# Attention units of 64 tokens of two batches, in array quarters, in place of 128 tokens of one

## The chip, the cores and the metric

The kernel runs on one core of a Trainium2 chip, as one program. The metric is the device time of a run in microseconds. All times below are of that one core.

## The reference

A linear attention with a decaying state, then two feed-forward layers. The first layer is a leaky rectifier with a slope per feature, the second the mish function.

```python
for t in range(S):                      # B, H, S, D = 4, 8, 768, 48
    cur = np.einsum('bhd,bhe->bhde', u[None] * kt, vt)
    y[:, :, t] = np.einsum('bhd,bhde->bhe', rt, state + cur)
    state = w[None, :, :, None] * state + np.einsum('bhd,bhe->bhde', kt, vt)
x = y as (3072, 384)
x = (relu(x @ w_in) + alpha * min(x @ w_in, 0)) @ w_out      # 384 -> 2048 -> 384
x = mish(x @ w2_in) @ w2_out                                 # 384 -> 2048 -> 384
```

## The kernel before

The sequence is cut into six chunks of 128 tokens. A unit of attention is one chunk of one batch, with all eight heads: 24 units, four to a block, blocks zero to five. Unit u is batch u % 4 of chunk u // 4. A block of four units gives 512 tokens of x, and the first layer works on 512 tokens at a time.

Inside a unit the decay is put into r and k beforehand (prep_rk multiplies both with the table RK). Then the unit is: the carried state T times r (first loop of batch, L324), scores k times r (L296, written for the unit after), which a masked copy on VectorE (L300) puts into A above a diagonal that ScalarE presets (L284), the unit's contribution to the state (L334; the keys for it are scaled with the table Kn on GpSimd, L276), and v times A (L339), which adds onto the carried part in the same PSUM banks. The two heads of a pair lie at partitions 0 to 47 and 64 to 111, so that carried state and scores run in quarters of the TensorE array (64 rows by 64 columns), four at a time; the state and v times A contract over 128 tokens and run in two halves. All these matmuls are in fp32, and each is shown by the trace as two records.

Afterwards t_decay (L345) and t_update (L352) bring T up to date on VectorE, x_parts splits y into a high and a low part (ScalarE L70, VectorE L73), and six small DMAs move the heads of the last pair into place in x. Block zero has functions of its own (c_first, attend0, x_first, states_first).

The first layer has 96 slots, six blocks times 16 weight blocks. A slot is nine matmuls into h (L144), the activation (L426, L428), its split (L70, L73) and nine matmuls into acc (L458) for the slot two before. In the first 16 slots each slot also prepares its weights: ScalarE scales (L96, L97), VectorE joins (L102) and takes the low part (L73), and the high part is a cast on ScalarE or GpSimd (L113).

The order of all this is written out by hand: `at(place, work, ...)` puts a step at a place counted in slots, and the steps run in the order of their places. Block zero's places are the table E, those of every later unit come from the offsets K in plan_unit, and AT gives each unit's slot: 2 for unit four, 5 for unit five, then one every four slots. The engines work through their instructions in that order. Loads stand on SyncE's queue (SP) in the same order. nat holds r, k and v of a unit by token; its three buffers set when the next load can start, and on GpSimd prep_c multiplies r, u and k (L267, L268).

```python
at(s + 0.60, batch, u)
at(s + 0.61, t_decay, u)
at(s + K["t"], t_update, u)
at(s + K["x"], x_parts, u)
```

Of the kernel before, what the change touches and what calls it, by code (L numbers as in the profile page):

```python
# [30 lines left out]
C = 128  # L31
# [12 lines left out]
UNITS = [(b, j) for j in range(NCH) for b in range(B)]  # L44
BLOCKS = [UNITS[4 * j:4 * j + 4] for j in range(NCH)]

# [5 lines left out]
def attention_and_two_ff(ctx: ExitStack, tc, rkT, nat, wT, ub, consts, w1, w2, alphaT, out):  # L52
# [99 lines left out]
    cst = att.tile([128, (1 + NPR) * C], F32, name="cst")  # L152
# [5 lines left out]
    inp = {}  # L158
    vz_t = {}

# [7 lines left out]
    def load_unit(u):  # L168
        if u < B:
            f = NF - 2 * B + 2 * u  # L170
            rk = per.tile([PR, 2, NPR, C], F32, tag=f"w{f}", name=f"w{f}u")
            n = per.tile([128, 4, DM], F32, tag=f"w{f + 1}", name=f"w{f + 1}u")
            by_seat(rk, rkT[u], slice(None))
            dma.dma_start(out=n[:, 1:3], in_=nat[u, :, 1:3])
            inp[u] = (rk, n, n[:, 2])
            vz_t[u] = n[:, 3].rearrange("s (q c e) -> s q c e", q=2, c=KC)
            return
        a = att.tile([PR, 2, NPR, C], F32, tag="rk", name="rk", bufs=3)
        by_seat(a, rkT[u], slice(None))
        n = att.tile([128, 3, DM], F32, tag="nat", name="nat", bufs=3)  # L180
        dma.dma_start(out=n, in_=nat[u])
        inp[u] = (a, n, n[:, 2])
# [3 lines left out]
    w128 = att.tile([PR, NPR], F32, name="w128")  # L186
    Kn = att.tile([128, NPR, 2, D], F32, name="Kn")
    T = att.tile([PR, B, NPR, 64], F32, name="T")
    def tables():
# [27 lines left out]
        mul(w128, iG[:, :, 0], G[:, :, 8])  # L217
        mul(uw, uw, wide(wt, 2))

    def table_Kn():  # L220
        kw = new("m")[0:PR].rearrange("d (p s) -> d p s", p=NPR)
        t = bank("acc2")
        for p in range(NPR):
            act.activation(out=kw[:, p, :], in_=RK[:, 1, p, :], func=AF.Copy, scale=w128[:, p:p + 1])
            pe.transpose(t[:, p * C:p * C + PR], kw[:, p, :], ident[:PR, :PR])
# [3 lines left out]


# [4 lines left out]
    LAST = (1, 2)  # L235
# [42 lines left out]
    def preset(u, h):  # L278

        if h == 0:  # L280
            A_t[u] = att.tile([128, 2, NPR, C], F32, tag="A", name="A", bufs=2)
        for j in range(NPR):
            p, q = HEAD[h, j]
            act.activation(out=A_t[u][:, h, j, :], in_=ident, func=AF.Copy, scale=c_t[u][1][:, 2 * p + q, :])  # L284

    def scores(u):

        rk = inp[u][0]
        if u == 0:
            sc_t["banks"] = [bank("sc", 2) for h in range(2)]  # L290
        sc_t[u] = sc_t["banks"]
        for j in range(NPR):
            for half in (1, 0):
                t0 = 64 * half if u else 0
                for h in range(2):
                    pe.matmul(sc_t[u][h][HALF[half], j * C + t0:(j + 1) * C], rk[ROWS[h], 1, j, HALF[half]],  # L296
                              rk[ROWS[h], 0, j, t0:], start=True, stop=True)

    def masked(u, q):
        dve.copy_predicated(A_t[u][:, q].rearrange("s p t -> s (p t)"), mask, sc_t[u][q])  # L300
# [13 lines left out]
    def batch(u):  # L314


        b, j = UNITS[u]
        rk, n, v = inp[u]
        A = A_t.pop(u)
        y = yt_t[u] = [bank("yt"), bank("h", 2)]  # L320
        for r in range(2):
            for h, q in ((0, 0), (1, 1), (0, 1), (1, 0)):
                i = 2 * q + r
                pe.matmul(y[h][64 * q:64 * q + 64, r * C:(r + 1) * C], T[ROWS[h], b, i, :], rk[ROWS[h], 0, i, :],  # L324
                          start=(r == 0), stop=False)
        if u + 1 < NU:
            scores(u + 1)
        if j < NCH - 1:
            st_t[u] = y[0][:, 2 * C:2 * C + NPR * D]
            for i in range(NPR):  # L330
                for h in range(2):
                    p, q = HEAD[h, i]
                    o = (2 * p + q) * D
                    pe.matmul(st_t[u][ROWS[h], i * D:(i + 1) * D], n[:, 1, o:o + D], v[:, o:o + D], start=False, stop=False)  # L334
        for p in PAIR:
            for q in range(2):
                o = (2 * p + q) * D
                h, i = SEAT[p, q]
                pe.matmul(y[h][ROWS[q], p % 2 * C:(p % 2 + 1) * C], v[:, o:o + D], A[:, h, i, :],  # L339
                          start=False, stop=(p in LAST))  # L340

    def t_decay(u):
        b, j = UNITS[u]
        if j < NCH - 1:
            dve.tensor_tensor(out=T[:, b, :, 0:D], in0=T[:, b, :, 0:D], in1=w128.unsqueeze(2).to_broadcast([PR, NPR, D]), op=ALU.mult)  # L345

    def t_update(u):
        b, j = UNITS[u]
        if j < NCH - 1:
# [35 lines left out]
    def x_parts(u):  # L385

        y = yt_t.pop(u)
        hi, lo = x_of(u)
        y3 = att.tile([128, 2, C], F32R, tag="y3", name="y3", bufs=1)
        parts = [(y3[0:PR, 0], y3[0:PR, 1], y[1][0:PR, C:2 * C]), (hi[0:PR, 2], lo[0:PR, 2], y[1][0:PR, 0:C]),  # L390
                 (hi[0:PR, 0:2], lo[0:PR, 0:2], y[0][0:PR, 0:2 * C].rearrange("d (c t) -> d c t", c=2))]
# [4 lines left out]
        x = x_t[u // 4][:, :, :, u % 4 * C:(u % 4 + 1) * C].bitcast(F32)  # L396
        for q in range(2):
            for c in range(KC):
                dma.dma_start(out=x[48 + 64 * q:64 + 64 * q, :, c, :],
                              in_=y3[64 * q + 16 * c:64 * q + 16 * c + 16].bitcast(F32))  # L400
# [423 lines left out]
```

## Time and profile before

| what | value |
|---|---|
| runs | 903.83, 905.57, 3040.05 us; median 905.57 |
| profiled execution, span from the first to the last instruction | 904.7 us |
| TensorE busy | 892.5 us (99%) |
| VectorE busy | 648.0 us (72%) |
| ScalarE busy | 629.9 us (70%) |
| GpSimd busy | 107.1 us (12%) |

For the profiled execution only the span is given. The median of the runs stands 0.9 us above it. Busy shares are over the whole span: attention and the first layer take about the first 500 us, the second layer the rest, and the engines differ much between them. PE is TensorE's matmuls, PEld its weight loads, DVE VectorE, ACT ScalarE, POOL GpSimd. A wait is put down to the engine whose signal came last.

### The profile page before, as it was taken

To read this page: it belongs to the slowest core of one execution; us is meant where nothing else is said; L and a number is where in the kernel's file an instruction comes from. 1 tells how busy PE (TensorE), PEld (TensorE's weight loads), DVE (VectorE), ACT (ScalarE), POOL (GpSimd) and SP (SyncE) were. 2 spreads that over 40 slices of the span, in tenths; PEclk is the share of its full clock that TensorE was granted. 3 is DMA by queue.
4 is the path that set the end of the run, shared out by engine and by line. 5 is a ranking of instruction groups with operands and counts; after the bars stand their busy time and mean duration, and the time that the engine had idled before them with its cause. 6 is when DMAs were issued, how large, how long until landed. Compare 5 with 4: busy or idle time off the path is not lost.

```text
span 904.7 us, 15208 instructions
## 1 busy us (share of the span) xinstructions
PE 892.5 (99%) x5724; PEld 767.5 (85%) x5724; DVE 648.0 (72%) x998; ACT 629.9 (70%) x1173; POOL 107.1 (12%) x89
## 2 busy tenths in 40 slices
PE   8899999999999999999999999999999999999998
PEld 8777788888888888888888898999999989989997
DVE  5699866666556666554665787787787787787875
ACT  4687745445545444553555798898898898998985
POOL 1522242122122311100001100000000000000000
PEclk9899999999999999999999999999999999999999
DMA  7973443434344433412532200200200200100000
GB/s 205 337 258 110 137 136 125 135 125 139 123 133 140 146 116 104 139 62 85 167 109 64 105 1 1 71 0 1 71 1 1 71 1 1 36 0 1 36 1 36
DMA packets 37290, 79.78 MB, mean 88 GB/s; under 512 B 6368, under 2 KB 24416, under 8 KB 37216
## 3 DMA queue, kind: packets, MB, share of 16 engines
q1 hardware_dynamic: 36624, 78.81, 27.0%
q8 instruction: 45, 0.74, 0.4%
q14 instruction: 29, 0.24, 0.1%
q10 hardware_dynamic: 592, 0.00, 0.0%
HBM read 61.09 MB, written 15.73 MB: 85 GB/s over the span
## 4 chain that ended last, share of the span: by engine, by line
PE 88%; ACT 4%; DVE 4%; DMA 2%; issue 1%; POOL 0%; ACTq 0%; SPq 0%; DVEq 0%; POOLq 0%
PE h L144 40%; PE acc L458 20%; PE acc L566 10%; PE sc L566 7%; PE yt L566 3%; PE sc L296 2%; PE yt L324 1%; ACT A L284 1%; PE h L339 1%; PE yt L339 1%; DMA w4r<-in_w 1%; DVE w L73 1%; PE yt L334 1%; DVE g L428 1%; DVE wj L102 1%
## 5 line engine op out<-in xcount | busy, mean ns | idle before, releaser
L144 PE MATMUL h<-x,w 128*128 128x512 f32 x1728 | 419.4, 391 | 3.3 <-DVE w L73 1.6
L144 PEld LDWEIGHTS h<-x,w 128*128 128x128 f32 x1728 | 323.5, 188 | 71.8 <-DVE w L73 2.8
L458 PE MATMUL acc<-ghi,w 128*128 128x512 f32 x516 | 175.3, 394 | 0.0
L458 PEld LDWEIGHTS acc<-ghi,w 128*128 128x128 f32 x516 | 96.8, 188 | 23.4 <-issue 3.0
L426 ACT ACTIVATE m<-h 128x512 f32<-128x512 f32 x96 | 57.2, 595 | 84.0 <-PE h L144 83.7
L70 ACT ACTIVATE ghi<-g 128x512 fp32r<-128x512 f32 x86 | 54.3, 632 | 83.5 <-DVE g L428 49.5
L428 DVE SCALAR_TENSOR_TENSOR g<-m,oma,h 128x512 f32<-128x512 f32 x96 | 71.6, 746 | 44.6 <-ACT m L426 41.9
L458 PE MATMUL acc<-glo,w 128*128 128x512 f32 x258 | 100.6, 390 | 0.0
L566 PE MATMUL acc<-w,ghiB 128*128 128x384 f32 x384 | 98.0, 336 | 0.0
L73 DVE TENSOR_TENSOR glo<-g,ghi 128x512 fp32r<-128x512 f32 x86 | 62.8, 730 | 47.8 <-ACT ghi L70 47.3
L514 DVE SCALAR_TENSOR_TENSOR a<-ghi,h 128x512 f32<-128x512 f32 x96 | 66.1, 688 | 36.2 <-ACT ghi L511 29.1
L514 DVE SCALAR_TENSOR_TENSOR g<-s,c 128x512 f32<-128x512 f32 x96 | 66.3, 691 | 21.8 <-ACT s L511 18.9
L70 ACT ACTIVATE ghiB<-g 128x512 fp32r<-128x512 f32 x106 | 65.8, 621 | 18.3 <-DVE g L514 7.8
L73 DVE TENSOR_TENSOR gloB<-g,ghiB 128x512 fp32r<-128x512 f32 x106 | 72.7, 686 | 7.8 <-ACT ghiB L70 7.8
L522 ACT ACTIVATE m<-h 128x512 f32<-128x512 f32 x96 | 56.0, 583 | 28.3 <-PE h L144 28.3
L511 ACT ACTIVATE ghi<-m,half 128x512 f32<-128x512 f32 x96 | 69.6, 725 | 3.2
L566 PEld LDWEIGHTS acc<-w,ghiB 128*128 128x128 f32 x384 | 69.7, 188 | 1.3
L511 ACT ACTIVATE glo<-ghi,m 128x512 f32<-128x512 f32 x96 | 68.1, 709 | 0.1
L511 ACT ACTIVATE s<-s,m 128x512 f32<-128x512 f32 x96 | 68.1, 709 | 0.0
L511 ACT ACTIVATE s<-glo,m 128x512 f32<-128x512 f32 x96 | 68.0, 709 | 0.0
L514 DVE SCALAR_TENSOR_TENSOR b<-ghi,a 128x512 f32<-128x512 f32 x96 | 67.4, 702 | 0.1
L514 DVE SCALAR_TENSOR_TENSOR c<-glo,b 128x512 f32<-128x512 f32 x96 | 65.8, 685 | 0.0
(168 smaller groups left out, 1205.9 us busy)
## 6 DMA issues: line engine op xcount, KB each, us to landing
wrawr<-in_w SPq DMA_DIRECT2D x24, 768.0 KB, 4.6
nat<-in_nat SPq DMA_DIRECT2D x20, 576.0 KB, 4.4
w2d<-wj SPq DMA_DIRECT2D x16, 384.0 KB, 2.5
wraw<-w2d SPq DMA_DIRECT2D x16, 384.0 KB, 3.1
rk<-in_rkT SPq DMA_DIRECT2D x40, 128.0 KB, 3.1
x2d<-xo SPq DMA_DIRECT2D x6, 768.0 KB, 4.0
x<-x2d SPq DMA_DIRECT2D x6, 768.0 KB, 4.9
out<-oo SPq DMA_DIRECT2D x24, 192.0 KB, 1.9
```

The lines of the kernel that those rows point to most:

```text
L70: act.activation(out=hi, in_=src, func=AF.Copy)
L73: eng.tensor_tensor(out=lo, in0=src, in1=hi.bitcast(F32), op=ALU.subtract)
L144: pe.matmul(h, w_in(layer, f, a, c), x[:, b, c, :], start=(k == 0), stop=(k == 3 * KC - 1))
L296: pe.matmul(sc_t[u][h][HALF[half], j * C + t0:(j + 1) * C], rk[ROWS[h], 1, j, HALF[half]], rk[ROWS[h], 0, j, t0:], start=True, stop=True)
L339: pe.matmul(y[h][ROWS[q], p % 2 * C:(p % 2 + 1) * C], v[:, o:o + D], A[:, h, i, :], start=False, stop=(p in LAST))
L426: act.activation(out=m, in_=hA[s], func=AF.Relu, scale=-1.0)
L428: dve.scalar_tensor_tensor(out=g, in0=m, scalar=oma[:, f:f + 1], in1=hA.pop(s), op0=ALU.mult, op1=ALU.add)
L458: pe.matmul(acc[0][c], w_out(0, f, a)[:, c * 128:(c + 1) * 128], g[b], start=(f == 0 and k == 0), stop=(f == NF - 1 and k == 2))
L511: act.activation(out=out, in_=in_, func=AF.Square, scale=scale, bias=fin[bias])
L514: dve.scalar_tensor_tensor(out=out, in0=in0, scalar=scalar, in1=in1, op0=op0, op1=ALU.mult)
L522: act.activation(out=bnew("t", n), in_=v["h", n], func=AF.Tanh, scale=0.5)
L566: pe.matmul(acc[1][t][:, :DM], g[a][:, t * C:(t + 1) * C], w_out(1, f, b), start=(f == 0 and k == 0), stop=(f == NF - 1 and k == 2))
```

## The change

From block one on (units 4 to 23) a unit is 64 tokens of two batches. Of a block's four units the first two are the two halves of the chunk for batches 0 and 1, the last two for batches 2 and 3. The 128 partitions of the token side are 64 tokens of one batch and 64 of the other, so every matmul of a unit stands in a quarter of the array. The state is carried every 64 tokens: t_decay and t_update work on two batches at once, and the first halves of block five also hand a state on. In batch the carried part is done in two groups, before the scores and after the state, and a memset of one unused column of T on GpSimd stands between. r and k are loaded and multiplied with RK once for two units (prep_pair), and the pad DMAs of x are issued once for two units. Kn and the mask get a copy of their halves at the start (half_Kn by DMA, half_tables on GpSimd). The states go to the score banks in place of the bank yt.

```diff
+def seat_of_unit(u):
+    j, r = divmod(u, 4)
+    return j, r // 2, r % 2
+
+def more_state(u):
+    j, _, half = seat_of_unit(u)
+    return j < NCH - 1 or half == 0
...
-        a = att.tile([PR, 2, NPR, C], F32, tag="rk", name="rk", bufs=3)
-        by_seat(a, rkT[u], slice(None))
+        j, bp, half = seat_of_unit(u)
+        if half == 0:
+            rk_t[j, bp] = [att.tile([PR, 2, NPR, C], F32, tag="rk", name="rk", bufs=4) for _ in range(2)]
+            for i in range(2):
+                by_seat(rk_t[j, bp][i], rkT[B * j + 2 * bp + i], slice(None))
         n = att.tile([128, 3, DM], F32, tag="nat", name="nat", bufs=3)
-        dma.dma_start(out=n, in_=nat[u])
+        for i in range(2):
+            dma.dma_start(out=n[HALF[i]], in_=nat[B * j + 2 * bp + i, HALF[half]])
...
+    def half_Kn():
+        dma.dma_start(out=Kn[HALF[0]], in_=Kn[HALF[1]])
...
+    def prep_pair(u, i):
+        rk = inp[u][0][i].rearrange("d i p (h t) -> d (i p) h t", h=2)
+        w = RK.rearrange("d i p t -> d (i p) t")[:, :, HC // 2:HC // 2 + HC]
+        dve.tensor_tensor(out=rk, in0=rk, in1=w.unsqueeze(2).to_broadcast([PR, 2 * NPR, 2, HC]), op=ALU.mult)
...
         for j in range(NPR):
-            for half in (1, 0):
-                t0 = 64 * half if u else 0
+            for i in (1, 0):
                 for h in range(2):
...
+                        rk = inp[u][0][i]
+                        s = t = HALF[half]
+                        o = slice(j * HC, (j + 1) * HC)
+                    pe.matmul(sc_t[u][h][HALF[i], o], rk[ROWS[h], 1, j, s], rk[ROWS[h], 0, j, t], start=True, stop=True)
...
     def batch(u):
...
-        for r in range(2):
-            for h, q in ((0, 0), (1, 1), (0, 1), (1, 0)):
-                i = 2 * q + r
-                pe.matmul(y[h][64 * q:64 * q + 64, r * C:(r + 1) * C], T[ROWS[h], b, i, :], rk[ROWS[h], 0, i, :],
-                          start=(r == 0), stop=False)
+        def carried(same):
+            for r in range(2):
+                for h, q in ((0, 0), (1, 1), (0, 1), (1, 0)):
+                    i, k, p = (h if same else 1 - h), 2 * q + r, 2 * h + r
+                    pe.matmul(y[i][64 * q:64 * q + 64, p * HC:(p + 1) * HC], T[ROWS[h], 2 * bp + i, k, :],
+                              pair[i][ROWS[h], 0, k, t], start=(r == 0 and not same), stop=False)
+        carried(False)
+        pool.memset(T[:, 2 * bp:2 * bp + 2, :, 63:64], 0.0)
         if u + 1 < NU:
             scores(u + 1)
-        if j < NCH - 1:
-            st_t[u] = y[0][:, 2 * C:2 * C + NPR * D]
-            for i in range(NPR):
-                for h in range(2):
+        if more_state(u):
+            st_t[u] = [t[:, NPR * HC:NPR * HC + NPR * D] for t in sc_t["banks"]]
+            nf = n.rearrange("s i d -> s (i d)")
+            for k in range(NPR):
+                for i, h in ((0, 0), (1, 1), (0, 1), (1, 0)):
...
+                    pe.matmul(st_t[u][i][HALF[h], k * D:(k + 1) * D], nf[HALF[i], DM + o:DM + o + 64], v[HALF[i], o:o + D],
+                              start=True, stop=True)
+        carried(True)
         for p in PAIR:
-            for q in range(2):
+            for i, q in ((0, 0), (1, 1), (0, 1), (1, 0)):
...
+                pe.matmul(y[i][ROWS[q], p * HC:(p + 1) * HC], v[HALF[i], o:o + D], A[HALF[i], h, k, :],
+                          start=False, stop=(p == PAIR[-1]))
...
+        parts = [(y3[0:PR, 0, i, HALF[half]], y3[0:PR, 1, i, HALF[half]], y[i][0:PR, 3 * HC:4 * HC]) for i in range(2)]
+        parts += [(x[0:PR, 0, :, i], x[0:PR, 1, :, i], y[i][0:PR, 0:3 * HC].rearrange("d (c t) -> d c t", c=KC))
+                  for i in range(2)]
...
-            at(n + K["r"], prep_rk, u + 2)
+            if seat_of_unit(u + 2)[2] == 0:
+                at(n + K["r0"], prep_pair, u + 2, 0)
+                at(n + K["r1"], prep_pair, u + 2, 1)
...
-        dma.dma_start(out=cst[:, 0:3 * C], in_=consts)
-        dma.dma_start(out=cst[:, 3 * C:], in_=consts[:, C:])
+        dma.dma_start(out=cst, in_=consts[:, 0:2 * C])
```

In the tables K loses r = -2.1 and gets r0 = -1.6 and r1 = -0.6. In E the two products of units 4 and 5 with RK (at -94.95 and 1.55) become the two of the pair (at -94.95 and 0.15), prep_kn of unit 4 goes from -95.4 to 0.1, and a step half at -94.44 (half_Kn, half_tables) is new.

TensorE's queue inside a unit of block one, before: the last scores of the unit after, the state (L334), v times A (L339), and the next group of the first layer (L458). The names in brackets are the engines and DMA queues waited for.

```order
L296 MATMUL sc<-rk 64x64 x2
L296 MATMUL sc<-rk 64x128 x2
L334 MATMUL yt<-nat 48x48 [waits DMAHW0_49,Pool_49]
L334 MATMUL yt<-nat 48x48 x7
L339 MATMUL h<-A,nat 48x128 x2
L339 MATMUL yt<-A,nat 48x128 x4
L339 MATMUL h<-A,nat 48x128 x2
```

The same place in the change: scores (now L337), state (L383), the second carried group (L369), the first of v times A (L390).

```order
L337 MATMUL sc<-rk 64x64 x4
L383 MATMUL sc<-nat 64x48 [waits Pool_49]
L383 MATMUL sc<-nat 64x48 x15
L369 MATMUL yt<-rk,T 64x64 [waits Pool_49]
L369 MATMUL h<-rk,T 64x64
L369 MATMUL yt<-rk,T 64x64
L369 MATMUL h<-rk,T 64x64
```

The state has 16 instructions for 8, none is 128 columns wide, half of the carried instructions moved behind the state, and the first of these waits for GpSimd.

GpSimd's queue around unit four, before: the keys of units 2, 4 and 3 scaled with Kn (L276), unit five's three products, two casts of weights, unit six.

```order
L276 TENSOR_TENSOR w13u<-w13u,Kn 128x384 [waits DMAHW2_49]
L276 TENSOR_TENSOR nat<-nat,Kn 128x384 [waits Pool_49]
L276 TENSOR_TENSOR w15u<-w15u,Kn 128x384 [waits DMAHW7_49]
L267 TENSOR_TENSOR nat<-nat,ubt 128x384 [waits DMAHW4_49]
L268 TENSOR_TENSOR nat<-nat 128x384 [waits Pool_49]
L276 TENSOR_TENSOR nat<-nat,Kn 128x384 [waits Pool_49]
L113 CAST w_642<-wj 128x768 [waits DVE_49]
L113 CAST w_794<-wj 128x768 [waits DMAHW0_49,DVE_49,Activation_49]
```

The same place in the change.

```order
L310 TENSOR_TENSOR w15u<-w15u,Kn 128x384 [waits DMAHW6_49]
L177 COPY cst<-cst 64x64 [waits DVE_49]
L179 COPY cst<-cst 64x64 [waits Pool_49]
L179 COPY cst<-cst 64x64
L310 TENSOR_TENSOR nat<-nat,Kn 128x384 [waits DMAHW4_49,Pool_49]
L301 TENSOR_TENSOR nat<-nat,ubt 128x384 [waits DMAHW5_49]
L302 TENSOR_TENSOR nat<-nat 128x384 [waits Pool_49]
L310 TENSOR_TENSOR nat<-nat,Kn 128x384 [waits Pool_49]
L125 CAST w_655<-wj 128x768 [waits DVE_49]
L373 MEMSET T 112x8 [waits PE_49]
L125 CAST w_824<-wj 128x768 [waits DMAHW7_49,DVE_49,Activation_49]
```

Unit four's keys now wait for a DMA (that of half_Kn) behind three small copies, and the memset of unit four's batch stands behind unit five's products and a cast that waits for VectorE.

## Rows read from the trace of the kernel before

**Rows 1.** The page's first part: busy us (share of the span) xinstructions.
```profile
PE 892.5 (99%) x5724; PEld 767.5 (85%) x5724; DVE 648.0 (72%) x998; ACT 629.9 (70%) x1173; POOL 107.1 (12%) x89
```
**Rows 2.** Busy time by stretch: from:to, length, PE, PEld, DVE, ACT, POOL, PEclk, DMA.
```profile
67.70:88.15 20.45, 19.81 (x155) 15.85 (x155) 18.84 (x27) 15.51 (x30) 6.13 (x6) 1.00 0.38 122
...
205.50:224.90 19.40, 19.40 (x153) 15.92 (x152) 12.75 (x20) 10.29 (x23) 5.11 (x3) 1.00 0.51 163
399.00:418.00 19.00, 19.00 (x148) 15.53 (x139) 8.75 (x14) 9.39 (x22) 0.00 (x0) 1.00 0.21 69
```
**Rows 3.** The chain of waits around a unit: start us, us, engine and what.
```profile
186.22 0.25 PE yt L324
...
186.82 0.87 PE sc L296 x24
187.69 0.49 PE yt L334 x16
...
189.06 2.27 PE acc L458 x9
191.33 2.04 PE h L144 x9
193.37 2.04 PE acc L458 x9
...
208.45 2.27 PE acc L458 x9
```
**Rows 4.** The timeline of that unit: start us, us, engine, line, operation.
```profile
186.31 0.27 PE L324 MATMUL yt<-rk,T 48*64 48x128 f32 x1
...
186.33 0.27 PE L324 MATMUL h<-rk,T 48*64 48x128 f32 x1
...
186.42 0.27 PE L324 MATMUL yt<-rk,T 48*64 48x128 f32 x1
...
187.62 0.56 PE L334 MATMUL yt<-nat 128*48 128x48 f32 x16
...
188.02 0.39 PE L339 MATMUL h<-A,nat 128*48 128x128 f32 x4
```
**Rows 5.** Busy time of L296 alone in one stretch: length, PE, PEld, clock, DMA.
```profile
186.64:187.07 0.43, 0.43 (x24) 0.43 (x26) 1.00 0.00 0
```
**Rows 6.** The timeline of GpSimd around unit four and from 194 us.
```profile
39.08 1.87 POOL L276 TENSOR_TENSOR nat<-nat,Kn 128x384 f32<-128x384 f32 x1
52.66 1.22 POOL L113 CAST w<-wj 128x768 fp32r<-128x768 f32 x1 [11.72 <-DVE wj L102]
...
194.81 1.02 POOL L267 TENSOR_TENSOR nat<-nat,ubt 128x384 f32<-128x384 f32 x1 [15.89 <-DMA nat<-in_nat]
195.90 1.61 POOL L268 TENSOR_TENSOR nat<-nat 128x384 f32<-128x384 f32 x1
```
**Rows 7.** GpSimd by line: xcount, busy us, mean ns of one, idle before.
```profile
L478 POOL MEMSET m<- 128x1 f32 x2 | 0.1, 101 | 0.0
```
**Rows 8.** VectorE by line, 60 to 480 us, same columns.
```profile
L300 DVE COPY_PREDICATED A<-cst,sc 128x512 f32<-128x512 uint32 x38 | 27.8, 732 | 0.0
...
L73 DVE TENSOR_TENSOR x<-yt,x 112x256 fp32r<-112x256 f32 x19 | 7.9, 415 | 0.0
L73 DVE TENSOR_TENSOR y<-h,y 112x128 fp32r<-112x128 f32 x19 | 5.5, 291 | 23.5 <-ACT x L70 21.6 <-DMA rk<-in_rkT 1.9
...
L345 DVE TENSOR_TENSOR T<-T,w 112x192 f32<-112x192 f32 x15 | 5.3, 351 | 0.0
```
**Rows 9.** The timeline of SP's queue.
```profile
35.91 3.69 SPq L90 DMA_DIRECT2D wrawr<-in_w  x3
```
**Rows 10.** DMA issues: xcount, KB each, median us to landing.
```profile
w9r<-in_w SPq DMA_DIRECT2D x1, 768.0 KB, 9.8
```
**Rows 11.** The chain of waits at the start.
```profile
9.61 0.59 SPq L174
...
10.24 7.27 DMA w4r<-in_w
```

More of the change, by code (lines that the diff above doesn't have):

```diff
@@ L42 @@
 HALF = (slice(0, 64), slice(64, 128))
-UNITS = [(b, j) for j in range(NCH) for b in range(B)]
-BLOCKS = [UNITS[4 * j:4 * j + 4] for j in range(NCH)]
+HC = C // 2
+NU = B * NCH
+def seat_of_unit(u):
[4 more added lines that the diff above has]
+    return j < NCH - 1 or half == 0
 MK = (32.0 / 768398401.0) ** 0.5
@@ L387, in x_parts @@
         y = yt_t.pop(u)
[L388 to L391, printed above, removed]
+        j, bp, half = seat_of_unit(u)
+        if j not in x_t:
+            x_t[j] = new_x()
+        x = x_t[j].rearrange("d i c (b t) -> d i c b t", b=B)[:, :, :, 2 * bp:2 * bp + 2, HALF[half]]
+        if half == 0:
+            y3_t[j, bp] = att.tile([128, 2, 2, C], F32R, tag="y3", name="y3", bufs=1)
+        y3 = y3_t[j, bp]
+        parts = [(y3[0:PR, 0, i, HALF[half]], y3[0:PR, 1, i, HALF[half]], y[i][0:PR, 3 * HC:4 * HC]) for i in range(2)]
+        parts += [(x[0:PR, 0, :, i], x[0:PR, 1, :, i], y[i][0:PR, 0:3 * HC].rearrange("d (c t) -> d c t", c=KC))
+                  for i in range(2)]
         for hi, _, t in parts:
@@ L395, in x_parts @@
             lo_of(dve, lo, hi, t)
[L396 to L400, printed above, removed]
+        if half == 1:
+            x = x_t[j].bitcast(F32)[:, :, :, 2 * bp * C:2 * (bp + 1) * C]
+            for q in range(2):
+                for c in range(KC):
+                    dma.dma_start(out=x[48 + 64 * q:64 + 64 * q, :, c], in_=y3[64 * q + 16 * c:64 * q + 16 * c + 16].bitcast(F32)
+                                  .rearrange("d i b t -> d i (b t)"))
     def pad_v(u):
@@ L657, in attention_and_two_ff @@
         dve.memset(uw, 0.0)
-        act.activation(out=w128, in_=uw[:, :, 0], func=AF.Prelu, scale=1.0, alpha=2.0)
+        act.activation(out=w96, in_=uw[:, :, 0], func=AF.Prelu, scale=1.0, alpha=2.0)
         for h, i in HEAD:
@@ L696, in attention_and_two_ff @@
             at(E["kn"][u], prep_kn, u)
+        at(E["half"][0], half_Kn)
+        at(E["half"][0], half_tables)
         at(E["st"][0], states_first, 0)
@@ L701, in attention_and_two_ff @@
                 at(place, work, (0, f), *{w_hi: (False,), w_lo: (dve,)}.get(work, ()))
-        for work, place in zip((prep_c, prep_rk, prep_kn, scores, prep_c2), E["u4"]):
-            at(place, work, B)
-        for work, place in zip((prep_c, prep_rk, prep_kn, prep_c2), E["u5"]):
+        for work, place in zip((prep_c, (prep_pair, 0), (prep_pair, 1), prep_kn, scores, prep_c2), E["u4"]):
+            work, *more = work if isinstance(work, tuple) else (work,)
+            at(place, work, B, *more)
+        for work, place in zip((prep_c, prep_kn, prep_c2), E["u5"]):
             at(place, work, B + 1)
```

71 lines of the change are left out of this document (41 added, 30 removed).

## The prediction

> **What bounds the kernel now.** I read the page's first part, then the chain of waits, then busy time by stretch, then single units. TensorE is busy for 892.5 us, 99% of the span [rows 1], and the chain of waits runs along it almost all the way. So what TensorE does not have to do is taken from the end, unless another engine steps in. Busy time by stretch shows where that could be [rows 2]: in a stretch of block one, from one attention unit to the next, VectorE is busy for 18.84 of 20.45 us and TensorE sits idle for 0.64; in block three TensorE has no idle time and VectorE is at 12.75 of 19.40. The granted clock is 1.00 in all of them, the 2.4 GHz level. So block one has two near bounds, the rest of the attention blocks one.
>
> The chain between two units shows the price of a unit [rows 3]. A slot without one is 2.04 + 2.04 = 4.08 us. From 189.06 to 208.45 are 19.39 us, four slots and one unit: 19.39 - 16.32 = 3.07 us. In the chain these are the carried state (L324) 0.60, from 186.22 to 186.82, of which 0.25 pass at its first start, scores (L296) 0.87, new state (L334) 0.49, values (L339) 0.88, from 188.18 to 189.06, and 2.27 instead of 2.04 for the next group of L458. In the last attention block, without new state, the period is 19.0 us [rows 2], so a unit there costs 2.7.
>
> What a round is: four matmuls in four quarters of the array start within 0.02 us (186.31 to 186.33), and the next four 0.11 us after the first (186.42) [rows 4]; an fp32 matmul has two records, so one instruction fills two rounds of its quarter. With 128 moving columns a round is 0.11 us. The new state has 16 records of 48 columns in two halves of the array, 8 rounds in 0.40 us (187.62 to 188.02), so 0.05 each. By straight line 64 columns take about 0.06.
>
> **The change part by part.**
>
> *TensorE, removed and added.* A unit's rounds were 4 (carried) + 8 (scores) + 8 (values) of 0.11 and 8 (state) of 0.05: 2.6 us, and 0.47 at the edges: about 0.16 as the first quarter round starts, 0.09 where scores go over to full-height state matmuls (0.49 for 0.40), 0.23 going back to L458. Now everything stands in quarters: 8 + 8 carried instructions are 4 + 4 rounds, 16 scores 8, 16 state 8, 16 values 8. That is 32 rounds at 0.06 = 1.92 us; the edge in the middle goes, 0.39 stays: 2.31 us, 0.76 less than 3.07.
>
> But a unit now is 64 instructions, 128 matmul and 128 weight-load records, where it was 80 and 80. Four quarters at 0.06 us want a record every 7.5 ns. No row shows that kept up: the densest stretch of scores has 24 matmuls and 26 loads in 0.43 us, 8.6 ns each [rows 5]. If that is the pace at which they can be handed out, a unit takes 256 x 0.0086 = 2.20 + 0.39 = 2.59 us. I take the middle, 2.45, a gain of 0.62; the ends 2.31 and 2.59 go into the range. Units of the last block: two of four now have a state for the second half, so (2.45 + 1.97) / 2 = 2.2 against 2.7, 0.5 less. Blocks two to four of attention: 12 x 0.62 = 7.4 us. Last: 4 x 0.5 = 2.0.
>
> *The memset of T's column 63.* It makes the second carried group wait for GpSimd, which waits for the first. What is queued behind the wait on TensorE is that group, the values, and with them x; ScalarE's y and x wait for those. Cover: scores and state between the groups, 16 rounds, 0.96 us (0.48 without state). Price of the trip: a last matmul of 0.27 us [rows 4], a small GpSimd memset of 0.10 [rows 7], and a start after a wait, 0.25 as at the unit's first matmul [rows 3]: 0.62. It fits, so nothing; were all of it bare, it would be 0.62 in each of 20 units, 12 us. It holds while GpSimd is free: the memset stands behind the two products of the unit after (L267 and L268, 1.02 + 1.61 us). Those started at 194.81, after 15.89 us of wait for nat, and ended at 197.5, 8 us before the unit at 205.5 [rows 6], so GpSimd is free from block two on; the third product moves behind the memset and has a whole period left.
>
> The Trainium skill (TensorEngine Tiling (Array Packing), Gotcha 1: PSUM Pressure) says that different row tiles may not use one PSUM bank at a time and that the program must see to it. In the diff each row half keeps to one bank in each group, and the memset parts the two carried groups, between which the banks are swapped; no run here shows the rule at work. By it the sum stays as it is.
>
> *VectorE and ScalarE.* Two masked copies of 512 columns (0.73 us each) become 256 columns; the nearest row is 0.42 for 112x256 [rows 8]: 0.62 less a unit. The split of y has four pieces for three: 2 x 0.35 (as 112x192) and 2 x about 0.25 against 0.42 and two of 0.29: 0.2 more. The decay of T covers two batches, 384 for 192 columns: between 0.35 and 0.73, take 0.2 more. Together 0.2 less a unit; the two products with RK now fall into every second gap. From block two on that lies beside a TensorE without gaps and costs nothing; in block one VectorE sets the period, so its units give 0.2 (between nothing and 0.62): 4 x 0.2 = 0.8 us. ScalarE's presets halve their columns, and it is the emptier of the two there, 15.5 of 20.45 us [rows 2]: nothing.
>
> *The copy of Kn's half by DMA.* It stands on SP behind three raw weights, issued until 39.6 now, and the transfer in its place now, w9r, takes 9.8 us to land [rows 9, 10]: about 49. GpSimd cannot scale unit four's keys before it lands (such a product takes 1.87 us; now the last of unit five is through at 40.9 [rows 6]), then come unit five's three products (1.02 + 1.61 + 1.87), the cast of w (1.22, now at 52.66), and only then unit four's memset, on which TensorE waits at about 53. From landing at 49 this ends at 56.6: 3.6 us of wait for TensorE, and the low weight part of VectorE behind the cast comes about as late. If it lands at once it costs nothing. I take half, 1.8.
>
> *Start.* One issue on SP is gone ahead of the first weights (such an issue takes 0.59 us, and w4r's transfer right behind is on the chain [rows 11]): 0.6 less.
>
> Sum: 7.4 + 2.0 + 0.8 - 1.8 + 0.6 = 9.0 us. The profiled span goes from 904.7 to 895.7. The median of the runs is 905.57, 0.9 above that span, so the median I expect is, rounded, **897**.
>
> **The rivals.**
>
> *All of it arrives* (2.31 us a unit, Kn early, block one follows TensorE): 16 x 0.76 + 4 x 0.67 + 0.6 = 15.4, or 890. For it: rounds at 128 columns follow each other without a gap and queues run ahead of the array. Against it: VectorE's 18.84 of 20.45 in block one [rows 2].
>
> *Matmuls cannot be handed out that fast, and the kernel gets slower.* Place: TensorE's own queue inside each unit. Sixteen state records of only 48 columns take 0.40 us, a start every 25 ns, over two halves of the array (187.62 to 188.02 [rows 4]). If 25 ns were a floor for any two starts kept up longer than the queue reaches, 128 of them take 3.2 + 0.39 = 3.59 us: 0.52 more than now in 18 units with state, and in the two without 112 x 25 ns = 2.8 + 0.39, 0.5 more than 2.7; the last block's two with state pay 0.9. 16 x 0.52 + 2 x 0.9 + 2 x 0.5 = 11, and 1.8 for Kn: the median would be 918, slower. It decides from 22 ns a start on (128 x 0.022 = 2.8). Against it: 24 matmuls that start in 0.43 us, 18 ns each [rows 5].
> The Trainium skill (TensorE: Matmul & The Clock Gate, Wait — 56ns, not 53.3ns?) states such a floor, about 25 ns from start to start however small the matmul is. The trace bounds it: over quarters four starts fall within 20 ns [rows 4], and over a stretch one comes every 18 ns [rows 5]; a longer one no row shows.
>
> *The quarters do not run side by side* (two only at a time): 64 rounds of 0.06 = 3.84 + 0.39 = 4.23 us, 1.16 more a unit, 23 us, or 929. Against it: carried state runs four side by side with the same rows and columns of the array [rows 4].
>
> *GpSimd comes late in block one*, 3 us at unit four and again at units five to seven, each behind a cast: about 5 us of the 9.0 lost, or 902.
>
> **How the numbers follow.** Forecast 0.47, all of it 0.22, GpSimd late 0.17, the 25 ns floor 0.09, no quarters 0.05. The range goes from 888 (all of it, and a little more) to 909 (late GpSimd together with 2.59 us a unit, and part of the floor's way). About 2% (18 us), what a measurement of this kernel tells from no change, lies at 887.5 below: even all of it stays above, so faster by over 2% has only what the ends of my rounds leave out, 0.1; slower by over 2% (923.7) is the last rival and some of the floor, 0.06; within 2% has 0.84.
>
> **What would show it.** The period from unit to unit in blocks two to four: 18.8 us (4 slots and 2.45), 18.6 if all arrives, 19.9 under the floor. Starts of one quarter 0.06 us apart through scores and state show rounds at the array's pace; growing gaps there show the hand-out. A wait of the second carried group for GpSimd should appear at unit four alone, with the Kn transfer and the cast ahead of it; at each unit it would prove me wrong. VectorE's share in block one should stay above 90%. I am wrong if the period of block two is over 19.4, or if block one loses over 4 us.

## The result and the profile after

The changed kernel takes 913.07 us (median of 4 runs, 909.47 to 913.74); the kernel before, on the same chip, 904.7. The ratio is 1.0097 (95% interval 1.0071 to 1.0123). It is about 8 us slower, where 9 us less were forecast, and lies outside the range. One of the four runs before took 3040.05 us, and the ratio leaves it out. The profiled execution has a span of 910.9 us.

The first part of its page answers to [rows 1]: TensorE is busy for less than before, and no longer for 99% of the span.

```profile
PE 883.9 (97%) x6684; PEld 761.3 (84%) x6684; DVE 636.3 (70%) x1025; ACT 623.2 (68%) x1193; POOL 90.2 (10%) x112
```

Where the time came from is read from the start of the first matmul of each slot of the first layer (L144 before, L156 now), in us of the span. The last two columns are two of the experiments below.

| slot | before | changed | difference | e9 | e10 |
|---|---|---|---|---|---|
| 0 | 41.57 | 38.75 | -2.8 | 38.27 | 38.00 |
| 1 | 47.13 | 45.15 | -2.0 | 47.61 | 45.77 |
| 3 (unit four before it) | 56.80 | 66.47 | +9.7 | 58.23 | 56.44 |
| 6 (unit five) | 72.83 | 84.58 | +11.8 | 76.32 | 72.07 |
| 10 (unit six) | 93.25 | 103.21 | +10.0 | 94.93 | 91.51 |
| 14 (unit seven) | 113.62 | 125.94 | +12.3 | 116.14 | 112.09 |
| 18 (unit eight) | 133.00 | 144.75 | +11.8 | 135.96 | 131.29 |
| 32 (second block boundary) | 199.32 | 210.25 | +10.9 | 201.22 | 195.24 |
| 48 | 276.87 | 286.21 | +9.3 | 276.90 | 269.61 |
| 64 | 354.42 | 362.16 | +7.7 | 353.12 | 343.99 |
| 80 | 429.65 | 435.78 | +6.1 | 426.78 | 417.52 |

From slot 18 on the change gains; all of the loss is made before that, most of it at unit four. (The start differs between executions: slot 0 lies between 36.30 and 41.57 in the profiles of this case.)

**A steady unit.** The stretch from one unit to the next in block three, by windows, is 18.59 us with TensorE busy in all of it and VectorE in 12.50; before it was 19.39 [rows 3]. The columns are those of [rows 2].

```profile
177.69:196.28 18.59, 18.59 (x201) 15.37 (x200) 12.50 (x21) 9.06 (x22) 3.25 (x4) 1.00 0.32 97
```

The timeline of TensorE through the next unit answers to [rows 4]: first carried group, scores, new state, second carried group.

```profile
196.32 0.27 PE L369 MATMUL h<-rk,T 48*64 48x64 f32 x1
...
196.60 0.65 PE L337 MATMUL sc<-rk 48*64 48x64 f32 x32
197.07 0.63 PE L383 MATMUL sc<-nat 64*64 64x48 f32 x32
...
197.52 0.23 PE L369 MATMUL yt<-rk,T 48*64 48x64 f32 x1
```

The 32 records of scores take 0.47 us (196.60 to 197.07), 14.7 ns each, and those of the new state, of 48 columns, 0.45. So a quarter fewer columns save next to nothing there; what sets that pace, no run shows. GpSimd's timeline has the memset between the two carried groups done at 196.99, 0.53 us before the second starts:

```profile
196.88 0.11 POOL L373 MEMSET T<- 112x8 f32 x1 [15.27 <-PE yt L369]
```

**Where TensorE waits.** The view of waits of the changed kernel (engine, line, waited for: us in total, times, longest):

```profile
PE sc L383 <- POOL nat L310: 6.7, 1, 6.7
PE yt L369 <- POOL T L373: 3.1, 2, 2.8
PE h L156 <- DMA x<-y: 2.7, 2, 1.3
PE sc L337 <- DVE A L341: 1.5, 2, 0.8
PE h L369 <- DVE g L487: 1.4, 2, 0.7
```

The first two are unit four (2.8 of the second). On SP, Kn's copy stands behind the eight rk and two nat loads of the third unit and three raw weights, and is issued at 45.20, not at 39.6 as the prediction had it:

```profile
30.63 11.59 SPq L186 DMA_DIRECT2D rk<-in_rkT  x8
42.26 1.24 SPq L206 DMA_DIRECT2D nat<-in_nat  x2
43.54 1.53 SPq L102 DMA_DIRECT2D wrawr<-in_w  x3
45.20 0.51 SPq L259 DMA_DIRECT2D Kn<-Kn  x1
```

Most of the 11.59 us for the eight rk loads is itself a wait. SP's own view of waits has:

```profile
SPq L186 <- DMA w6r<-in_w: 2.8, 1, 2.8
SPq L186 <- DMA w7r<-in_w: 2.1, 1, 2.1
SPq L186 <- DMA nat<-in_nat: 1.4, 2, 0.8
```

The fifth of these loads is issued at 36.3, as w6r lands (issued at 27.77, 8.5 us to land), and w6r is the eighth transfer before it on the queue; the last three follow the landings of the two nat loads and of w7r in the same way. In all fourteen profiles of this case no transfer is issued while eight others are in flight, counting SP's and ScalarE's together. So these four loads are held on SP until older ones have landed.

GpSimd waits 17.10 us for the copy and starts at 56.01; the copy took 10.7 us to land. Then its whole queue follows, product by product, the cast, and only then the memset:

```profile
56.01 0.99 POOL L310 TENSOR_TENSOR nat<-nat,Kn 128x384 f32<-128x384 f32 x1 [17.10 <-DMA Kn<-Kn]
56.96 0.99 POOL L301 TENSOR_TENSOR nat<-nat,ubt 128x384 f32<-128x384 f32 x1
...
60.04 0.83 POOL L125 CAST w<-wj 128x768 fp32r<-128x768 f32 x1
60.80 0.12 POOL L373 MEMSET T<- 112x8 f32 x1
```

The third row is a wait for the pad DMAs of x at two block boundaries (at the first, slot 32, the mark names a piece of VectorE that ends at the same time); the last two are units five and seven, which wait for VectorE twice each.

**The clock.** In windows of 4 us the granted clock falls from 1.00 to 0.50 (2.4 to 1.2 GHz) after TensorE has stood idle in unit four, and is 1.00 again from 67 to 71. The last three columns are the clock, the share of the DMA engines and GB/s.

```profile
47.00:51.00 4.00, 3.38 (x60) 2.54 (x58) 2.22 (x3) 2.25 (x5) 0.00 (x0) 1.00 0.98 333
51.00:55.00 4.00, 0.00 (x0) 0.00 (x0) 0.00 (x0) 2.05 (x3) 0.00 (x0) 0.73 1.02 375
55.00:59.00 4.00, 1.11 (x32) 0.95 (x32) 0.00 (x0) 0.00 (x0) 2.91 (x3) 0.50 0.99 404
59.00:63.00 4.00, 2.03 (x49) 1.84 (x50) 2.64 (x4) 1.48 (x7) 1.84 (x4) 0.50 0.15 58
63.00:67.00 4.00, 4.00 (x12) 3.08 (x11) 1.84 (x5) 1.62 (x7) 0.00 (x0) 0.56 0.76 197
```

The same rows bear on the late landing: the DMA engines are full from 47 to 59 (0.98 to 1.02), and what was issued around the copy lands in the order of issue, the third raw weight (issued at 44.64) 10.6 us after its issue, at 55.3, and the copy at 55.9.

The clock falls again behind the waits of units five and seven:

```profile
79.00:83.00 4.00, 3.92 (x116) 3.49 (x117) 3.62 (x6) 4.00 (x12) 0.53 (x1) 0.64 0.15 40
123.00:127.00 4.00, 4.00 (x22) 3.17 (x15) 3.25 (x8) 3.19 (x14) 0.62 (x1) 0.81 0.53 147
```

### The profile page after: what moved, and what is told of

Same layout as the page of the kernel before. It is cut to its first block, busy times and chain, and to the rows that moved or that the text cites. A ratio compares the mean times of both kernels' runs of the same rounds, so it can differ in the third digit from the quotient of the medians.

```text
span 910.9 us, 17108 instructions
## 1 busy us (share of the span) xinstructions
PE 883.9 (97%) x6684; PEld 761.3 (84%) x6684; DVE 636.3 (70%) x1025; ACT 623.2 (68%) x1193; POOL 90.2 (10%) x112
## 4 chain that ended last, share of the span: by engine, by line
PE 86%; DVE 3%; ACT 2%; issue 1%; DMA 1%; POOL 0%; SPq 0%; DVEq 0%; ACTq 0%; POOLq 0%
PE h L156 40%; PE acc L517 20%; PE acc L625 10%; PE sc L625 7%; PE yt L625 3%; PE sc L337 1%; PE sc L383 1%; PE yt L390 1%; PE h L369 1%; DVE rk L280 1%; PE yt L369 1%; DMA x<-y 1%; POOL w L125 0%; SPq L458 0%; ACT ghi L82 0%
## 5 line engine op out<-in xcount | busy, mean ns | idle before, releaser
L156 PE MATMUL h<-x,w 128*128 128x512 f32 x1728 | 419.7, 392 | 6.2 <-DMA x<-y 2.7
L156 PEld LDWEIGHTS h<-x,w 128*128 128x128 f32 x1728 | 323.4, 188 | 76.1 <-issue 5.6
L517 PE MATMUL acc<-ghi,w 128*128 128x512 f32 x516 | 178.1, 399 | 0.0
L487 DVE SCALAR_TENSOR_TENSOR g<-m,oma,h 128x512 f32<-128x512 f32 x96 | 71.5, 745 | 64.2 <-ACT m L485 63.9
L82 ACT ACTIVATE ghi<-g 128x512 fp32r<-128x512 f32 x86 | 54.3, 631 | 77.4 <-PE acc L517 55.3
L85 DVE TENSOR_TENSOR glo<-g,ghi 128x512 fp32r<-128x512 f32 x86 | 60.8, 707 | 57.7 <-ACT ghi L82 57.7
```

The source lines that it names most:

```text
L82: act.activation(out=hi, in_=src, func=AF.Copy)
L85: eng.tensor_tensor(out=lo, in0=src, in1=hi.bitcast(F32), op=ALU.subtract)
L156: pe.matmul(h, w_in(layer, f, a, c), x[:, b, c, :], start=(k == 0), stop=(k == 3 * KC - 1))
L487: dve.scalar_tensor_tensor(out=g, in0=m, scalar=oma[:, f:f + 1], in1=hA.pop(s), op0=ALU.mult, op1=ALU.add)
L517: pe.matmul(acc[0][c], w_out(0, f, a)[:, c * 128:(c + 1) * 128], g[b], start=(f == 0 and k == 0), stop=(f == NF - 1 and k == 2))
```

## The experiments

My account after this look: the quarters give all they can, and three losses take it back: Kn's copy with the clock's fall behind it (11.7 us), the pads of x behind the loads on SP (about 1.5 us at each of three boundaries), and the place of the second product of a pair on VectorE in block one (some 4 us). The rivals are that VectorE sets block one anyway, so that removing a wait only uncovers the next, and that the memset's handshake costs time in each unit.

Gains below are differences of medians from the change (913.07); each ratio is to runs of the kernel before taken beside the experiment. Where an interval overlaps that of the change (1.0071 to 1.0123), as in e3 and e4, the time alone does not decide, and a stretch of the trace does.

**e1, the copy early, on ScalarE's queue.**

```diff
-        dma.dma_start(out=Kn[HALF[0]], in_=Kn[HALF[1]])
+        for h in HALF:
+            act.dma_start(out=Kn[h], in_=Kn0[HALF[1]])
...
-        at(E["half"][0], half_Kn)
+        at(E["Kn"][0] + 0.001, half_Kn)
```

Kn0 is block zero's own table, in a buffer (y3) that is free at that time.

> Edit: the copy of Kn's half is issued from ScalarE's queue as soon as the table Kn stands, and block zero scales its keys with a table of its own, so that the copy waits for nothing else. Theory (the 11.7 us that unit four loses come from the copy behind the loads on SP): GpSimd's wait of 17.1 us for it goes, TensorE's 7.3 us gap between scores and new state goes, of the 3.1 us before the second carried group some stay because the cast of a weight still stands ahead of the memset; the granted clock keeps its 2.4 GHz level there. Time 902 to 906. Rival (VectorE sets the period of block one anyway, the wait only stood in front of it): less than 4 us come back, 909 or more, with the idle time before slot 3 now ended by VectorE.

Measured: 908.33 us, ratio to before 1.0047 (1.0025 to 1.0069), between theory and rival. GpSimd no longer waits for Kn and the gap at unit four is gone: slots 1 to 3 take 10.2 us (21.3 in the change, 9.7 before). But slots 0 to 1 take 11.4 us (6.4 in the change): on SP the first eight rk loads now take 11.80 us to issue (6.30), everything behind them is later, and GpSimd waits for nat until 39.60. SP's view of waits names what holds them, the two copies, which land 7.6 and 9.1 us after their issue on ScalarE's queue and are among the eight in flight:

```profile
SPq L186 <- DMA Kn<-Kn: 6.7, 2, 6.0
```

e9 is the test without this side effect.

**e2, the pads ahead of the loads.**

```diff
-            at(s + 0.63, load_unit, u + 3)
+            at(s + K["x"] + 0.001, load_unit, u + 3)
```

> Edit: the loads of unit u+3 are issued behind the six pad DMAs of x of unit u, not ahead of them. Theory (at three block boundaries, slots 32, 48 and 64, TensorE waits about 1.5 us for the pads, which stand behind eight rk loads on SP): these three waits go, 4 to 5 us, 908 to 909. Rival (the pads are late because y itself is late, or because the transfers are): under 1 us, 912 to 913. A loss would show that loads that now stand behind the pads come late (raw weights and nat in block one).

Measured: 908.21 us, ratio 1.0049 (1.0029 to 1.0069), 4.9 us less, as the theory has it. The changed kernel's SP and TensorE before slot 48, from their timelines: the pads are issued until 285.24, TensorE's last matmul of acc starts at 284.48, and the next block of x at 286.21.

```profile
274.00 5.98 SPq L186 DMA_DIRECT2D rk<-in_rkT  x8
280.09 1.17 SPq L206 DMA_DIRECT2D nat<-in_nat  x2
281.37 3.87 SPq L458 DMA_DIRECT2D x<-y  x6
```

```profile
284.48 0.39 PE L517 MATMUL acc<-ghi,w 128*128 128x512 f32 x1
286.21 2.06 PE L156 MATMUL h<-x,w 128*128 128x512 f32 x8 [1.34 <-DMA x<-y]
```

With the edit the order on SP is turned round, and no wait for the pads is left:

```profile
274.22 3.87 SPq L458 DMA_DIRECT2D x<-y  x6
278.19 5.11 SPq L186 DMA_DIRECT2D rk<-in_rkT  x8
```

From slot 44 to 48 it takes 18.60 us (264.14 to 282.74), as any other period, where the change took 20.09.

**e3, the products of a pair one slot earlier.**

```diff
-r0=-1.6, r1=-0.6
+r0=-2.6, r1=-1.6
```

> Edit: the two products of a pair with RK move one slot ahead on VectorE (r0 from -1.6 to -2.6, r1 from -0.6 to -1.6). Theory (units five and seven lose 2.0 and 2.3 us because the second product, 2.02 us, stands ahead of the join of a weight and the masked copy): those two lose nothing, with the clock staying up 3 to 4 us come back, 909 to 910. Rival (VectorE is full in block one, so the place of the product in its queue only moves the wait): 912 to 914.

Measured: 909.09 us, ratio 1.0068 (1.0038 to 1.0099), 4.0 us less by the medians. From slot 3 to 18 it takes 75.03 us, and 73.98 to 75.47 in the four later kernels with this edit; in the seven profiles of the change and its variants without it, 77.05 to 78.32 (before: 76.20). The means lie 3.0 us apart. VectorE's timeline before unit five in the changed kernel: the product, 2.02 us, holds up the activation's second half (L487), the join and the masked copy; the carried state (77.85) and the scores (79.08) wait for them.

```profile
75.11 2.02 DVE L280 TENSOR_TENSOR rk<-rk,RK 112x1024 f32<-112x1024 f32 x1
77.06 0.73 DVE L487 SCALAR_TENSOR_TENSOR g<-m,oma,h 128x512 f32<-128x512 f32 x1
77.72 0.95 DVE L114 SCALAR_TENSOR_TENSOR wj<-wrawr 128x768 uint32<-128x768 uint32 x1
78.59 0.43 DVE L341 COPY_PREDICATED A<-cst,sc 128x256 f32<-128x256 uint32 x1
```

In e3 the granted clock stays at 1.00 from 75 to 83, where the change has 0.64 from 79 to 83. So VectorE was not simply full in block one; the product stood in the wrong place.

**e4, TensorE kept busy while it waits.** The 30 matmuls go to a bank that nothing reads.

```diff
             scores(u + 1)
+        if u == B:
+            t2 = bank("acc0")
+            for _ in range(30):
+                pe.matmul(t2[:, 0:C], ident, ident, start=True, stop=True)
```

> Edit: while TensorE waits in unit four for the new state's keys it runs 30 matmuls of 128 columns into a free bank (about 6.6 us of the 7.3 us gap), which are not used. The wait itself stays. It prices the clock: if the fall of the granted clock to 1.2 GHz from 52.9 to 66.5 us costs the 2 to 3 us that the slower groups there suggest (4.0 for 2.2 us, 1.02 for 0.56), the time is 910 to 911; if the engines beside TensorE set that stretch, 913 as before.

Measured: 909.23 us, ratio 1.0071 (1.0040 to 1.0102), 3.8 us less by the medians, 2.4 by the ratios. The clock stays at 1.00:

```profile
51.00:55.00 4.00, 4.00 (x77) 3.93 (x78) 1.24 (x2) 2.53 (x4) 0.00 (x0) 1.00 1.03 372
```

What the clock costs is read from the start of unit four's memset to slot 3, the same work in both kernels, first in the change, then here:

```profile
60.80:66.47 5.67, 5.50 (x58) 4.49 (x58) 3.93 (x8) 1.72 (x8) 0.12 (x2) 0.50 0.44 118
60.32:63.53 3.21, 3.05 (x58) 2.56 (x59) 3.12 (x8) 1.72 (x8) 0.11 (x2) 1.00 0.22 57
```

That is 2.5 us. In e2, e3, e5 and e8, at 0.50 to 0.52, it takes 5.52 to 5.66; in e1, e7, e9 and e10, at 1.00, 3.17 to 3.21. From slot 1 to slot 3 e4 takes 17.0 us instead of 21.3, but 1.9 of these 4.4 us are GpSimd's, which starts on unit four's keys 8.9 us after slot 1 in place of 10.9. So of unit four's loss 2.5 us are the lower clock, within the 2 to 3 expected, and the rest is the wait.

**e5, the third unit's loads behind the copy.**

```diff
-        load_unit(B + 2)
         more_raw(7)
...
         at(E["half"][0], half_Kn)
+        at(E["half"][0], load_unit, B + 2)
```

> Edit: the loads of r, k and v for the third unit in the pair order (eight rk and two nat for units six and seven) are issued on SP behind the three raw weights and the copy of Kn, not ahead of them; the copy itself is as in the change. Theory (Kn comes late because SP still issues these ten loads, 12.8 us, ahead of it): Kn lands some 10 us earlier, GpSimd's wait of 17.1 us falls below 6, TensorE's gap at unit four nearly goes with the clock staying up, and nothing is late at the start as it was in the profiled run with the early copy: 901 to 904. Rival (the transfer itself is slow behind the raw weights in the DMA queues, wherever it is issued): 906 to 910, with Kn landing 10 us after its issue.

Measured: 905.87 us, ratio 1.0014 (0.9990 to 1.0038), 7 us less, but the theory's numbers for the copy do not hold: SP issues it only 4.6 us earlier (it waits there for GpSimd's product of unit three, which reads the old half until 40.6), and it still takes 12.3 us to land.

```profile
40.59 0.51 SPq L259 DMA_DIRECT2D Kn<-Kn  x1
```

```profile
53.01 1.01 POOL L310 TENSOR_TENSOR nat<-nat,Kn 128x384 f32<-128x384 f32 x1 [11.69 <-DMA Kn<-Kn]
```

The rival is right on the transfer: wherever it is issued among these loads, it lands late (in e6, with the same loads, it is issued at 36.39 and lands 9.7 us later). These rows do not account for the whole 7 us: e5's profiled execution is the slowest of its ten, 910.37 us.

**e6, e5 with e2 and e3**, and **e7, e6 with the copy as in e1.**

> Edit: the late loads, the pads ahead of the loads, and the products of a pair one slot earlier, all three. If they are separate losses their gains add up: 9 to 11, 5 and 4 us from 913 give 893 to 896. If block one is bound by VectorE, the first and the third overlap: 897 to 900, which is still under the kernel before.

> Edit: as the three together, with the copy of Kn also issued from ScalarE's queue as soon as the table stands. If the late loads already remove the wait for Kn, this adds nothing: within 2 us of the three. If Kn's landing behind the raw weights is what is left, it gives 2 to 4 us more.

Measured: e6 898.42 us, ratio 0.9930 (0.9905 to 0.9954); e7 901.16 us, ratio 0.9961 (0.9942 to 0.9980). The three together are faster than the kernel before. The gains of e5, e2 and e3 add up to 16.1, which makes 897; so they are three losses and not one, though the time fell in the band I had given to the rival, because e5 itself gave less than I had put. e7 is 2.7 us slower than e6 where I expected no loss, with overlapping intervals: slots 0 to 1 take 16.0 us there (7.4 in e6). It shares with e1 the copies on ScalarE's queue, and again one rk load waits on SP for such a copy, 7.4 us. The second eight take 15.39 us, as they wait for the landings of w6r, two nat loads, w7r and three raw weights.

**e8, nine memsets in place of one.**

```diff
-        pool.memset(T[:, 2 * bp:2 * bp + 2, :, 63:64], 0.0)
+        for _ in range(9 if u >= 2 * B else 1):
+            pool.memset(T[:, 2 * bp:2 * bp + 2, :, 63:64], 0.0)
```

> Edit: from block two on nine memsets of T's column instead of one stand between the two carried groups, so GpSimd's answer comes about 0.5 us later (a second instruction starts 0.06 us after the first). My account: the memset's trip is hidden behind scores and state, in block three the one memset ends at 196.99 and the second group starts at 197.52, so 0.5 us of the cover is unused: a unit's period stays at 18.6 us, or grows by at most 0.1. Rival (the handshake already costs time in each unit): the period grows by the whole 0.5 us, 16 units or 8 us in all.

Measured (one run): 924.46 us. My size was off, nine take 1.46 us, 1.35 more than one:

```profile
197.86 1.46 POOL L374 MEMSET T<- 112x8 f32 x9 [14.66 <-PE yt L369]
```

The second carried group starts at 199.37, 0.05 after them, and a period is 19.5 us (slots 32 to 40 from 211.87 to 250.90, two units), 0.9 more than 18.59. Of 1.35 us the first 0.5 cost nothing, all beyond costs in full. This is the account's cover of 0.53 us, and not the rival's whole price: one memset costs nothing.

**e9, Kn's halves without a DMA.** The same small products on TensorE and ScalarE that make the table make both halves, at the copy's place.

```diff
-        dma.dma_start(out=Kn[HALF[0]], in_=Kn[HALF[1]])
+        t = bank("acc0")
+        for p in range(NPR):
+            for h in HALF:
+                pe.matmul(t[h, p * C:p * C + PR], Kn_t["kw"][:, p, HALF[1]], ident[:PR, :PR], start=True, stop=True)
...
+            act.activation(out=Kn[:, 2 * h:2 * h + 2].rearrange("s r q d -> s q r d"), in_=tv[:, :, :, rows], func=AF.Copy)
```

> Edit: no DMA for Kn's halves at all. TensorE turns the upper half of the same table into both halves (8 small matmuls at the place of the copy), ScalarE writes it, block zero has a table of its own; loads, pads and products stand as in the change. Theory (the copy's late landing is what unit four loses, 11.7 us with the clock): GpSimd does not wait for Kn, TensorE goes from slot 1 to slot 3 in 10 to 11 us (21.3 in the change, 9.7 before): 901 to 904. Rival (the rk loads of two batches hold SP for 6 to 12 us each, so the weights of the first slots and the second unit's nat are late too, and the copy only hid this): 905 to 908, with waits for VectorE's joins or for nat in its place.

Measured: 903.09 us, ratio 0.9994 (0.9977 to 1.0011), 10.0 us less by this one edit (9.3 by the ratios), and within the theory's band. Slots 1 to 3 take 10.6 us. GpSimd is through with unit five's keys before the wait used to end, and waits for the join of a weight only:

```profile
39.61 1.02 POOL L321 TENSOR_TENSOR nat<-nat,Kn 128x384 f32<-128x384 f32 x1
...
44.04 1.87 POOL L321 TENSOR_TENSOR nat<-nat,Kn 128x384 f32<-128x384 f32 x1
53.89 1.22 POOL L125 CAST w<-wj 128x768 fp32r<-128x768 f32 x1 [7.99 <-DVE wj L114]
55.06 0.11 POOL L384 MEMSET T<- 112x8 f32 x1
```

A new wait stands in its place, and the rival has a part in that: slots 0 to 1 take 9.3 us (6.4), as TensorE waits for VectorE's second product of the pair, and the granted clock falls to 0.51 (47 to 51).

```profile
45.10 1.14 PE L348 MATMUL sc<-rk 48*64 48x64 f32 x32 [4.50 <-DVE rk L291]
```

**e10, e9 with e5's late loads, e2 and e3**, and **e11, e10 with the cast of weight block three on ScalarE** (POOL_HI from 5 on).

> Edit: as e9, with the late loads, the pads ahead of the loads and the products of a pair one slot earlier. In the run with these three TensorE still waited 2.6 us in unit four for the memset behind Kn's landing (46.25 us). If that is all that is left of the copy: 2 to 3 us under the three's 898.4, 895 to 897. If the joins of the weights come no earlier: as the three, 898 to 899.

> Edit: as e10, and the cast of weight block three, which stands on GpSimd ahead of unit four's memset, runs on ScalarE. If the cast's 0.8 to 1.2 us ahead of the memset are bare: up to 1 us less than e10. If ScalarE's copy is as late (both wait for the join on VectorE), or ScalarE is late for it elsewhere: the same within 0.5 us, or up to 1 us more.

Measured: e10 894.48 us, ratio 0.9905 (0.9880 to 0.9929); e11 895.74 us, 0.9925 (0.9901 to 0.9950). e10 beats both kernels, 9.4 us under the one before and 18.6 under the change; e9, e2 and e3 by themselves add up to 18.9. The time is half a microsecond under the 895 to 897 expected. TensorE's 2.6 us of wait for unit four's memset in e6 are down to 0.4, and what is left in block one is VectorE:

```profile
PE sc L348 <- DVE rk L291: 3.6, 1, 3.6
PE h L156 <- DVE w L85: 2.8, 4, 1.1
...
PE yt L380 <- POOL T L384: 0.7, 2, 0.4
```

The cast's place (e11) makes no difference that the intervals show.

**e12, the kernel before with the change's mask alone.** It tests the term for the start.

```diff
-        dma.dma_start(out=cst[:, 0:3 * C], in_=consts)
-        dma.dma_start(out=cst[:, 3 * C:], in_=consts[:, C:])
+        dma.dma_start(out=cst, in_=consts[:, 0:2 * C])
```

> Edit on the kernel before: only the mask as in the change, 128 columns read once for each pair, so that one load of constants (131 KB in place of 197 and 131 KB) and one issue on SP fall away at the start; units stay 128 tokens of one batch. The prediction put 0.6 us on it (one issue, 0.59 us). In the changed kernel's profiled runs the first slot starts 1.4 to 5.3 us earlier than in the kernel before (41.57). If that comes from this load: slot 0 at 39.5 or earlier and 902 or less against 904 for the kernel before. If it comes from something else of the change or from the spread of the start: within 1 us of the kernel before.

Measured: 902.22 us against 903.29, ratio 0.9991 (0.9973 to 1.0010). Its profiled slot 0 starts at 37.01 (41.57 before), but the median is only 1 us lower: most of that difference is the spread of single executions.

## Why the prediction was wrong

**The step that failed is the copy of Kn's half by DMA.** It was put at 1.8 us with 3.6 as the most; e9 takes it out and gains 10.0. Of its three parts two were wrong. The issue: 39.6 was the place of w9r in the kernel before [rows 9], but the ten loads of the third unit, which the change doubles, stand ahead of it and wait themselves for older transfers to land, and it was 45.20. The landing: 9.8 us [rows 10] was good (10.7), so it came at 56, not 49. And what follows from it: the term ended with TensorE's wait of 3.6 us, which stood at 6.7 + 2.8, and had nothing for the clock, 2.5 us by e4. Taking half of 3.6, for a copy that might land at once, had no row behind it: in all nine kernels with the copy it landed 7.5 to 12.3 us after its issue.

**SP was priced for the start only.** At a block boundary the pads of x now stand behind eight rk and two nat loads in place of four and one, 7.4 us of issue. The prediction followed each moved product, but not this queue; e2 puts the omission at 4.9 us (from slot 32 to 64 it takes 148.75 us, the change 151.91).

**Block one** was to gain 0.8 us because VectorE sets its period. It lost: from slot 3 to 18, units five to eight, the changed kernel takes 78.28 us for 76.20 before, while four units at 0.80 could have gained 3.2. The cause is not VectorE's load, whose 19.11 us from 67.70 to 88.15 answer to 18.84 before [rows 2], but the place of a product of 2.02 us that before stood a slot and a half earlier, and the lower clock behind the waits for it (e3, 3.0 us of this stretch). The rival of a late GpSimd named units four to seven; unit four was late as it says, with 9.5 us of wait for its 3, and five and seven were late by VectorE.

**The units from block two on were right in kind and too small in size.** A period is 18.59 us, a gain of 0.80 where 0.62 was taken; a unit costs 2.27, even under the lower end of 2.31. Twelve units give 9.6 us (7.4 forecast), the last block 1.6 from slot 64 to 80 (2.0 forecast). The middle between 2.31 and 2.59 was the wrong choice: the 8.6 ns a record read from [rows 5] was the pace of a longer round, not of the hand-out, for records of scores now start every 14.7 ns with a weight load beside each, 7.3 ns a piece.
The Trainium skill (TensorE: Matmul & The Clock Gate, Wait — 56ns, not 53.3ns?) puts the least distance of two starts at about 25 ns. Over four quarters this trace does not show it, with 32 starts in 0.47 us; the rival that rested on it is out. (Two sums of rivals have slips that change nothing in their order: a unit without state has 96 matmul records and not 112, 0.8 us in all under that rival, and the last block's unit gains 0.63 and not 0.67 if all arrives.)

**The memset** was covered as worked out (0.62 us for the trip against 0.96): e8 finds 0.5 us to spare. **Start**: 0.6 us agrees with e12 (0.9991), whose interval does not part it from zero.

The forecast's 9.0 us are, then, near what the change gives once the three losses are mended (e10: 9.4), and the change as it stands loses about twice as much against e10. That the two numbers lie so close is partly luck: in e10 the units from slot 18 to 80 give 10.4 us, where 9.4 were forecast, and up to slot 18 it still takes 93.29 us from slot 0, 1.9 more than before, where the sum had a loss of 1.0 (0.8 - 1.8).

## What to carry to other kernels

Before a faster inner step is priced, list per queue (SP's, GpSimd's, VectorE's) what is issued ahead of each thing that the step waits for, with the new sizes: here a copy and six pads behind doubled loads, and one product that moved, cost more than the step gained. A load that takes long to issue may be waiting for an older one to land. A one-off copy by DMA at the start landed 7.5 to 12.3 us after its issue here; the same table made on TensorE and ScalarE cost no wait for it. And price an idle TensorE twice, as the wait and as the slower clock after it.

## What was not expected of the hardware

A gap of 6.7 us in TensorE cost 2.5 us more behind it, as the granted clock stood at 0.50 up to slot 3 at 66.47; with matmuls in the gap that nobody reads it stayed at 1.00 (e4).

Never more than eight transfers were in flight, SP's and ScalarE's together, in the fourteen profiles. So eight loads on SP took from 5.1 us (e2) to 16.84 us (e10) to issue, by what had still to land, and two copies on ScalarE's queue held up SP's loads (e1, 6.7 us). Whether the chip or the program's semaphores set the eight, no run shows.

VectorE's and GpSimd's instructions stretch where they run side by side. With GpSimd waiting, the second product of unit four's pair took 1.22 us (42.40 in the changed kernel); in e9, with GpSimd's products in the same 2 us, it took 2.02, and theirs 1.59 and 1.87 in place of 0.99:

```profile
41.36 1.75 DVE L114 SCALAR_TENSOR_TENSOR wj<-w6r 128x768 uint32<-128x768 uint32 x1
43.03 2.02 DVE L291 TENSOR_TENSOR rk<-rk,RK 112x1024 f32<-112x1024 f32 x1
```

So removing GpSimd's wait made VectorE later, which is part of the 4.5 us that e9 waits for it. By lines, the decay of T takes 1.09 us in the mean in the changed kernel, where 0.55 was its length alone (62.44) and forecast.
The Trainium skill (SBUF — State Buffer, SBUF: two separate sides) has these two engines share a pair of ports under an exclusive lock, where one waits for the other's whole instruction. The rows agree that both lose; that one stands still for the other's whole length, they do not show.

Left open: what the 3.6 us that e10 still waits for VectorE would give if they went, and what sets the pace of the new state's 48 columns.
